# A Fourier mixing and GELU kernel: the spill of the first stage in four parts, and DMA issues held to their slots by tiny transfers

## The chip, the cores and the metric

The kernel runs on one core of one Trainium2 chip. The metric is the device time of one execution in microseconds (us). Before the change it is 1863.5 us, the median of 3 runs (1861.09 to 1864.88). The profile is of a further execution.

## The reference

```python
def _attn_ref(x):                      # x: (8, 3008, 256) float32
    X = np.fft.fft(x, axis=1)
    X = np.fft.fft(X, axis=2)
    return X.real.astype(np.float32)

def _moe_ref(x, w_in, w_out):          # w_in: (256, 2048), w_out: (2048, 256)
    h = x @ w_in
    g = h * (1.0 / (1.0 + np.exp(-1.702 * h)))
    return (g @ w_out).astype(np.float32)

# reference: x = _attn_ref(x).reshape(8 * 3008, 256); return _moe_ref(x, w_in, w_out)
```

For each of 8 batches the real part of a two-dimensional Fourier transform is taken over sequence and channels; each of the 24064 rows then passes a layer with 2048 hidden channels, the sigmoid form of GELU and a second layer.

## The kernel before

**The stages of a batch.** The sequence of 3008 is split as 47 by 64. The **first stage** transforms over the 47: GpSimd folds pairs of rows of the tile xt (`fold1`, lines 208 to 229), TensorE multiplies by tables (`mix1`, line 231), and ScalarE copies the result back into slots of xt (line 256). `mix1` runs in four groups; group m fills the slots 4m to 4m+3 of xt. The result lies in the wrong order for the next stage, so it is written to a scratch tensor Td in DRAM (`spill`, line 326) and read back with other partitions (`fill`, line 331) into the tile t4. `rotate` (line 336) adjusts one column of it, and the **second stage** (`stage2`, line 343) transforms over the 64 for one of three blocks of a batch, into the tile pq. One row of pq goes through DRAM as well (`nyquist_out`, Nd<-pq, line 377) and comes back as a tile nb on all partitions (`nyquist`, line 368).

The input of a batch comes in two ways. `load_x` (line 197) reads it into xt in four pieces, each of two DMAs: one from x itself (512 or 240 KB), one from Xr (as many). Xr holds half of the rows in reversed order and is made by `turn` (line 187), a DMA from DRAM to DRAM in three pieces (752, 705 and 47 KB).

**The main loop.** The two layers are the bulk of the work. They run in 384 steps: 8 batches of 48, and a batch is 3 blocks of 16 steps, each for two of the 16 parts of the hidden channels and a half of a block's columns. In step t, TensorE's `begin` makes the hidden values of the next step in PSUM; ScalarE's `forward` (line 586) applies GELU to the values of step t and writes them into a ring of four places in the tile big (`at_left`, line 518); DVE and ScalarE make the values of the mirrored rows (`backward`, `activate_back`, lines 544 and 593); GpSimd and DVE form sums and differences (lines 601 to 630); TensorE's `product` and `small_products` (lines 182 and 664) multiply them by the second layer's weights three steps later. After 8 steps DVE transposes the results and SyncE stores them (`turned`, `store`, lines 716 and 802). The first 8 steps of batch 0 take a simpler form.

**How the order is set.** The schedule is manual: each engine executes its instructions in the order of the program, and semaphores join the engines. Stages of the next batch are hung into the steps of this one by `at(t, fn, ...)`: the function is called at the end of step t. Below, "slot k" of a batch is step 48b + k. In `begin` and the other functions TensorE, ScalarE, DVE and GpSimd have work in every step, so slots hold them in place. SyncE issues the DMAs, apart from a few at the start and the end, and has an instruction only where a DMA is to be issued. It waits where the data or the place of a DMA isn't ready, or for the completion of the DMA eight places earlier, whose semaphore it uses again; otherwise it goes on to the next DMA in the program's order, whatever its slot. The slots of the moved DMAs in batch b (`late` is 5 in batch 0 and 0 in the others):

- `turn` of batch b+2: slots 11, 12, 13
- `mix1` of batch b+1: slots 11, 15, 19 and 23, plus `late` (one of them a step more in batch 0)
- `spill` of batch b+1: slots 24 and 25, plus `late`; one DMA each for half of the partitions, with 16 slots of xt, 16 KB in one piece for each partition
- `fill` of batch b+1: slots 28, 29, 30, plus `late`
- `load_x` of batch b+2: slots 32, 34, 36, 38, plus `late`
- `rotate` of batch b+1: slot 36 (39 in batch 0); `stage2`: slots 8, 24 and 40, `nyquist_out` and `nyquist` in the two slots behind each

Of the kernel before, what the change touches and what calls it, by code (L numbers as in the profile page):

```python
# [27 lines left out]
F32 = mybir.dt.float32  # L28
# [7 lines left out]
NJ = NB // 2  # L36
NM = 48
# [9 lines left out]
def view(ap, offset, *dims):  # L47
    return bass.AP(ap.tensor, ap.offset + offset, [list(d) for d in dims])
# [63 lines left out]
def kernel(ctx: ExitStack, tc, x, w_in, w_out, tab1, tab2, out):  # L112
    nc = tc.nc
    B, S, D = x.shape
    DF = w_in.shape[1]
    H = D // 2
    NF = DF // 128
    NBLK = NG // 4
# [11 lines left out]

    Xr = [nc.dram_tensor(f"Xr{b}", (NA, NJ, D), F32, kind="Internal").ap() for b in range(B)]
    Nd = nc.dram_tensor("Nd", (B * NBLK, 512), F32, kind="Internal").ap()
    Td = [nc.dram_tensor(f"Td{b}", (NG * 128, D), F32, kind="Internal").ap() for b in range(B)]

    w1 = const.tile([128, (NJ + 3) * NM + 64 - NM], F32, tag="w1", name="w1")
# [15 lines left out]
    big = cv.tile([128, 19 * 1024], F32, tag="big", name="big")  # L151
# [33 lines left out]
    xt = xp.tile([128, NJ, D], F32, tag="x", name="xt")  # L185
# [137 lines left out]
        for _ in range(n):  # L323
            nc.tensor.matmul(ps[:], lhsT=wcs[0][:, 0:128], rhs=wcs[0][:, 0:512], start=True, stop=True)

    def spill(b, c):

        nc.sync.dma_start(out=view(Td[b], 16 * c * D, [NJ * D, NM], [1, 16 * D]),
                          in_=xt[64 * c:64 * c + NM, 0:16, :].rearrange("p q d -> p (q d)"))

    def fill(b, a0=0, a1=NG):
        if a0 == 0:
# [42 lines left out]
    def nyquist_out(b, blk):  # L375
        i = b * NBLK + blk
        nc.sync.dma_start(out=Nd[i:i + 1, :], in_=pqt[b, blk][0:1, 1, :])

    raw = {}

# [109 lines left out]
    A11, A21, S3, S2 = range(4)  # L490
# [27 lines left out]
    def at_left(t, q):  # L518
        return LEFT + t % 4 * 1024 + q * 256
# [311 lines left out]
    for e in odds:  # L831
# [7 lines left out]
                      in_=view(tab1, 0, [tab1.shape[1], 128], [28 * NM, 2], [1, ends]))  # L839
# [70 lines left out]
    def at(t, fn, *args):  # L910
        extra.setdefault(t, []).append((fn, args))
# [22 lines left out]
    for b in range(B):  # L934
        t0 = b * NBLK * NF
        late = 0 if b else 5
        if b + 2 < B:
            for k in range(3):
                at(t0 + 11 + k, turn, b + 2, k)
        if b + 1 < B:  # L940
            for c in range(NCH):
                for part in range(2):
                    at(t0 + 6 + 2 * c + part + late, fold1, b + 1, c, part, nc.gpsimd)
                if c % 2:
                    at(t0 + 9 + 2 * c + late + (late > 0 and c == 5), mix1, b + 1, c // 2)
            for c in range(2):
                at(t0 + 24 + c + late, spill, b + 1, c)
            for blk in range(NBLK):
                at(t0 + 28 + blk + late, fill, b + 1, 4 * blk, 4 * blk + 4)
            if b + 2 < B:  # L950
                for k in range(4):
                    at(t0 + 32 + 2 * k + late, load_x, b + 2, k)
            at(t0 + 36 + 3 * (late > 0), rotate, b + 1)
        for blk in range(NBLK):
            nxt = (b, blk + 1) if blk + 1 < NBLK else (b + 1, 0)
            if nxt[0] < B:
                at(t0 + blk * NF + 8, stage2, *nxt)
                at(t0 + blk * NF + 9, nyquist_out, *nxt)
                at(t0 + blk * NF + 10, nyquist, *nxt)
# [109 lines left out]
```

## Time and profile before

| what | before |
|---|---|
| timed runs, median of 3 | 1863.5 us (1861.09 to 1864.88) |
| profiled execution, its own time | 1870.22 us |
| its span, first to last instruction | 1868.4 us |
| mean granted TensorE clock | 0.998 |
| TensorE matmul busy | 1845.4 us, 99% |
| VectorE (DVE) busy | 1524.2 us, 82% |
| ScalarE (ACT) busy | 1150.3 us, 62% |
| GpSimd (POOL) busy | 962.7 us, 52% |
| SyncE waiting for the transposes ahead of the stores | 1245.3 us |
| bytes moved by DMA | 105.29 MB, mean 56 GB/s |
| DMAs of t<-Td (512 KB), of Td<-xt (768 KB) | 22, 14 |
| DMAs of xt<-x and of xt<-Xr (512 KB, 240 KB) | 14 and 14 of each |

PE is TensorE's matmul, PEld its weight load, which overlaps it. A row of waits names the waiting engine, its output and line, what it waited for, and then the total in us, the times and the longest one; "issue" stands for idle time in which the engine waited for no semaphore that the profile knows. A row of a timeline gives the start and the length in us, the engine, the line, the operation, output<-input and the count. A row of windows gives the stretch, then each engine's busy time with its instructions, the granted clock of TensorE, the mean busy share of the 16 DMA engines and the rate. The DMA view gives for each queue the packets, the megabytes and the share of the 16 engines' time; q1 is SyncE's queue, and the queues of kind "instruction" bring the engines' own instructions.

### The profile page before, as it was taken

How to read it: one execution, taken by the hardware profiler on the slowest of the kernel's cores; microseconds unless marked ns; L12 is line 12 of the kernel's file. 1: busy time of each engine (PE TensorE's matmuls, PEld its weight loads, DVE VectorE, ACT ScalarE, POOL GpSimd, SP SyncE). 2: the span in 40 equal slices, each digit the busy share in tenths (PEclk: the TensorE clock that was granted, in tenths of full speed). 3: DMA queues.
4: the chain of work that ended last, by engine and by line, in shares of the span. 5: the costliest groups of instructions: out<-in, count | busy, mean ns of one | idle time of the engine just before them, and what ended most of it. 6: DMA issues, size and time to landing. Idle time of an engine off the chain costs nothing.

```text
span 1868.4 us, 55818 instructions
## 1 busy us (share of the span) xinstructions
PE 1845.4 (99%) x23684; PEld 1413.1 (76%) x23684; DVE 1524.2 (82%) x2229; ACT 1150.3 (62%) x2248; POOL 962.7 (52%) x1057
## 2 busy tenths in 40 slices
PE   8999999999999999999999999999999999999998
PEld 5677777778777777777777777776877777778776
DVE  7888788888798877987789878887788888878874
ACT  6656666666666656666565666665666666656663
POOL 4676345744367434773348634475335754434442
PEclk9999999999999999999999999999999999999999
DMA  8720351125110350114302251112411021100011
GB/s 262 194 52 17 81 96 32 33 63 107 25 51 14 85 95 14 51 22 113 61 13 61 45 110 31 24 52 63 91 30 25 19 62 35 30 18 14 21 21 24
DMA packets 145690, 105.29 MB, mean 56 GB/s; under 512 B 105163, under 2 KB 128235, under 8 KB 144258
## 3 DMA queue, kind: packets, MB, share of 16 engines
q1 hardware_dynamic: 144226, 101.20, 24.8%
q8 instruction: 187, 3.06, 0.7%
q10 hardware_dynamic: 1216, 0.52, 0.1%
q14 instruction: 61, 0.50, 0.1%
HBM read 64.41 MB, written 48.05 MB: 60 GB/s over the span
## 4 chain that ended last, share of the span: by engine, by line
PE 87%; DVE 6%; ACT 3%; POOL 1%; DMA 1%; issue 1%; SPq 0%; DVEq 0%; ACTq 0%; POOLq 0%
PE x L182 32%; PE o L182 25%; PE low L664 23%; PE o L664 4%; DVE big L630 2%; PE ps L354 1%; PE ps L253 1%; DVE big L765 1%; DVE big L544 1%; DMA big<-in_moe_w_in_dram 1%; ACT x L571 1%; DMA wo<-in_tab_dram 0%; ACT big L586 0%; ACT g L583 0%; PE psw L182 0%
## 5 line engine op out<-in xcount | busy, mean ns | idle before, releaser
L601 POOL TENSOR_TENSOR big<-big 128x256 f32<-128x256 f32 (+1 forms) x376 | 348.2, 926 | 846.5 <-ACT big L593 742.1
L182 PE MATMUL x<-pq,wcs 128*64 128x256 f32 (+1 forms) x6016 | 773.9, 378 | 3.3 <-ACT g L583 2.2
L630 DVE TENSOR_TENSOR big<-big 128x512 f32<-128x512 f32 (+1 forms) x736 | 637.9, 881 | 35.0 <-PE low L664 18.0
L182 PE MATMUL o<-big,wo 128*64 128x256 f32 (+1 forms) x4800 | 623.1, 376 | 0.0
L182 PEld LDWEIGHTS x<-pq,wcs 128*64 128x64 f32 x6016 | 414.4, 137 | 190.7 <-issue 15.0
L182 PEld LDWEIGHTS o<-big,wo 128*64 128x64 f32 x4800 | 344.9, 137 | 144.4 <-DVE big L608 0.5
L583 ACT ACTIVATE g<-x 128x512 f32<-128x512 f32 (+1 forms) x376 | 221.8, 590 | 373.7 <-PE x L182 372.6
L544 DVE TENSOR_TENSOR big<-g,x 128x512 f32<-128x512 f32 (+2 forms) x440 | 253.8, 588 | 200.0 <-ACT big L586 199.7
L664 PE MATMUL low<-big 128*64 128x128 f32 (+1 forms) x5888 | 382.8, 271 | 3.8 <-issue 3.8
L664 PEld LDWEIGHTS low<-big 128*64 128x64 f32 x5888 | 337.8, 137 | 32.2 <-issue 3.9
L571 ACT ACTIVATE x<-nb,af 128x256 f32<-128x256 f32 (+1 forms) x752 | 352.7, 469 | 12.2
L602 POOL TENSOR_TENSOR big<-big 128x256 f32<-128x256 f32 (+1 forms) x376 | 358.8, 954 | 0.0
L586 ACT ACTIVATE big<-x 128x512 f32<-128x512 f32 (+1 forms) x376 | 220.6, 587 | 200.9 <-PE x L182 191.6
L593 ACT ACTIVATE big<-big 128x512 f32<-128x512 f32 (+1 forms) x376 | 231.8, 617 | 42.2 <-DVE big L544 40.3
L664 PE MATMUL low<-big,wo 128*64 128x128 f32 (+1 forms) x2944 | 221.2, 271 | 0.1
L664 PEld LDWEIGHTS low<-big,wo 128*64 128x64 f32 x2944 | 172.9, 137 | 3.8 <-DVE big L630 0.4
L609 DVE TENSOR_TENSOR big<-big 128x512 f32<-128x512 f32 (+1 forms) x188 | 147.7, 786 | 6.5
L608 DVE TENSOR_TENSOR big<-big 128x512 f32<-128x512 f32 (+1 forms) x188 | 136.8, 728 | 5.5 <-POOL big L601 5.5
L765 DVE TENSOR_TENSOR big<-big,low 128x512 f32<-128x512 f32 (+3 forms) x184 | 109.1, 610 | 3.4
L664 PEld LDWEIGHTS o<-big,wo 128*64 128x64 f32 x1472 | 92.7, 137 | 24.5
L664 PE MATMUL o<-big,wo 128*64 128x128 f32 (+1 forms) x1472 | 110.3, 270 | 0.0
L225 POOL TENSOR_TENSOR xt<-xt 111x510 f32<-111x510 f32 x56 | 76.1, 1360 | 4.4
(102 smaller groups left out, 965.8 us busy)
## 6 DMA issues: line engine op xcount, KB each, us to landing
out_dram<-os SPq DMA_DIRECT2D x284, 64.0 KB
t<-Td SPq DMA_DIRECT2D x22, 512.0 KB
Td<-xt SPq DMA_DIRECT2D x14, 768.0 KB
xt<-in_x_dram SPq DMA_DIRECT2D x14, 512.0 KB
xt<-Xr SPq DMA_DIRECT2D x14, 512.0 KB
nb<-Nd SPq DMA_DIRECT2D x23, 256.0 KB
out_dram<-os SPq DMA_DIRECT2D x96, 56.0 KB
Xr<-in_x_dram SPq DMA_DIRECT2D x7, 752.0 KB
```

Source lines behind the costliest of these rows:

```text
L182: nc.tensor.matmul(out[c0:c0 + 64], lhsT=lhs[:, c0:c0 + 64], rhs=rhs, skip_group_check=True, **how)
L544: nc.vector.tensor_tensor(free(out, at + m - 1, [by, 2], [RUN, blocks], [-1, m]), *ins, op=op)
L571: nc.scalar.activation(x[:, i * 256:i * 256 + n], nbt[b, blk][:, hh * 256:hh * 256 + n], ACTF.Copy, scale=af1[:, f:f + 1])
L583: nc.scalar.activation(two(g[:], n), two(xb[t][:], n), ACTF.Copy, scale=2.0)
L586: nc.scalar.activation(front(t), two(xb[t][:], width(t)), ACTF.Gelu_apprx_sigmoid)
L593: nc.scalar.activation(back(t), back(t), ACTF.Gelu_apprx_sigmoid)
L601: eng.tensor_tensor(right(t, S1, n), left(t, A21, n), right(t, A22, n), op=ALU.add)
L602: eng.tensor_tensor(left(t, S3, n), left(t, A11, n), left(t, A21, n), op=ALU.subtract)
L608: eng.tensor_tensor(s2, s1, a11, op=ALU.subtract)
L609: eng.tensor_tensor(s4, a12, s2, op=ALU.subtract)
L630: nc.vector.tensor_tensor(out, i0, i1, op=how)
L664: nc.tensor.matmul(o, lhsT=lhs, rhs=rhs, start=first_in, stop=(p == NP - 2), skip_group_check=True)
```

## The change

The spill is cut in four. `spill` takes a third argument q and moves the four slots of xt that the group q of `mix1` has filled, for half of the partitions, in pieces of 4 KB. Its two DMAs are issued one slot after the group, so that a batch has eight of them at slots 12, 16, 20 and 24 (plus `late`), where it had two.

A new function `paced(t)` issues a DMA of one element: from the place in big that `forward(t)` writes in that step, to a new scratch tensor Tk that nobody reads. SyncE has to wait for `forward(t)` before it issues it, and so do the DMAs behind it. The place is written again by `forward(t + 4)`. A `paced` stands ahead of each `turn`, each `fill` and each `load_x` of the main loop. The fills and the loads have moved one slot forward, to 27, 28, 29 and to 31, 33, 35, 37 (plus `late`).

```diff
+    Tk = nc.dram_tensor("Tk", (B * NBLK * NF, 1), F32, kind="Internal").ap()
...
-    def spill(b, c):
+    def spill(b, c, q):
 
-        nc.sync.dma_start(out=view(Td[b], 16 * c * D, [NJ * D, NM], [1, 16 * D]),
-                          in_=xt[64 * c:64 * c + NM, 0:16, :].rearrange("p q d -> p (q d)"))
+        nc.sync.dma_start(out=view(Td[b], (16 * c + 4 * q) * D, [NJ * D, NM], [1, 4 * D]),
+                          in_=xt[64 * c:64 * c + NM, 4 * q:4 * q + 4, :].rearrange("p q d -> p (q d)"))
...
+    def paced(t):
+        nc.sync.dma_start(out=Tk[t:t + 1, :], in_=big[0:1, at_left(t, A11):at_left(t, A11) + 1])
...
         if b + 2 < B:
             for k in range(3):
+                at(t0 + 11 + k, paced, t0 + 11 + k)
                 at(t0 + 11 + k, turn, b + 2, k)
         if b + 1 < B:
             for c in range(NCH):
                 for part in range(2):
                     at(t0 + 6 + 2 * c + part + late, fold1, b + 1, c, part, nc.gpsimd)
                 if c % 2:
-                    at(t0 + 9 + 2 * c + late + (late > 0 and c == 5), mix1, b + 1, c // 2)
-            for c in range(2):
-                at(t0 + 24 + c + late, spill, b + 1, c)
+                    k = t0 + 9 + 2 * c + late + (late > 0 and c == 5)
+                    at(k, mix1, b + 1, c // 2)
+                    for half in range(2):
+                        at(k + 1, spill, b + 1, half, c // 2)
             for blk in range(NBLK):
-                at(t0 + 28 + blk + late, fill, b + 1, 4 * blk, 4 * blk + 4)
+                at(t0 + 27 + blk + late, paced, t0 + 27 + blk + late)
+                at(t0 + 27 + blk + late, fill, b + 1, 4 * blk, 4 * blk + 4)
             if b + 2 < B:
                 for k in range(4):
-                    at(t0 + 32 + 2 * k + late, load_x, b + 2, k)
+                    at(t0 + 31 + 2 * k + late, paced, t0 + 31 + 2 * k + late)
+                    at(t0 + 31 + 2 * k + late, load_x, b + 2, k)
             at(t0 + 36 + 3 * (late > 0), rotate, b + 1)
```

## The prediction

> **What bounds the kernel now.** I read the page's busy line first, then the chain, then PE's own waits after the start-up, then two stretches of the same work, one batch apart.
>
> ```profile
> PE 1845.4 (99%) x23684; PEld 1413.1 (76%) x23684; DVE 1524.2 (82%) x2229; ACT 1150.3 (62%) x2248; POOL 962.7 (52%) x1057
> ...
> PE 87%; DVE 6%; ACT 3%; POOL 1%; DMA 1%; issue 1%; SPq 0%; DVEq 0%; ACTq 0%; POOLq 0%
> ```
>
> TensorE works 99% of the span and carries the chain, so a DMA edit can give back only what PE loses to a DMA. PE's waits from 85 to 1850 us are three groups (us in total, times, longest):
>
> ```profile
> PE low L664 <- issue: 3.8, 1, 3.8
> PE x L182 <- ACT g L583: 2.2, 6, 0.4
> PE x L182 <- ACT x L571: 0.4, 2, 0.2
> ```
>
> One wait of 3.8 us stands alone, and "issue" means that no semaphore explains it. From the ends of the forward activation (L586) in the trace I took each step's length. Batches 1, 2, 3, 4 and 6 last 225.11 to 225.13 us. Batch 5 lasts 231.78, and the whole 6.66 lies in its steps 25 and 26: 9.99 and 6.00, against 4.63 and 4.70 in the others. The windows show it (PE busy, PEld, DVE, ACT, POOL, granted clock, DMA share, GB/s); the first two rows are batch 5, the others the same work 225.1 us earlier:
>
> ```profile
> 1300.40:1304.20 3.80, 0.04 (x2) 0.03 (x2) 0.00 (x0) 1.81 (x4) 1.40 (x2) 0.84 0.26 89
> 1304.20:1308.80 4.60, 4.60 (x28) 3.90 (x29) 1.35 (x3) 0.60 (x1) 0.00 (x0) 0.50 0.39 119
> ...
> 1075.30:1079.10 3.80, 3.80 (x46) 2.67 (x44) 2.09 (x4) 2.71 (x6) 1.42 (x2) 1.00 0.32 92
> 1079.10:1083.70 4.60, 4.60 (x74) 4.02 (x72) 3.34 (x6) 2.73 (x7) 1.67 (x2) 1.00 0.34 118
> ```
>
> PE stands for 3.8 us and then runs at a granted clock of 0.50 for 4.6 us: 28 matmuls where the other batch has 74. What it waited for is its own instructions. The page counts 187 packets of instructions on q8; in the trace each has 16384 bytes, so one comes every 10 us. From 1282.5 to 1301.5 the DMA view has none:
>
> ```profile
> q8 instruction: 187, 3.06, 0.7%
> ...
> q1 hardware_dynamic: 2055, 2.04, 51.8%
> q14 instruction: 1, 0.01, 0.2%
> ```
>
> The packet due at 1293.0 (they normally start about 0.9 us before PE reaches the 256th instruction after the last) starts at 1302.0, 9.0 late, ends at 1303.0, and PE runs on at 1304.2. SyncE's timeline says what stood in front, and shows the other crowd, the loads of x, which belong to slots 32, 34 and 36 but are issued within 4 us:
>
> ```profile
> 1291.62 0.79 SPq L328 DMA_DIRECT2D Td<-xt  x2
> ...
> 1335.20 0.45 SPq L203 DMA_DIRECT2D xt<-in_x_dram  x1
> 1335.70 0.64 SPq L203 DMA_DIRECT2D xt<-Xr  x1
> 1336.38 0.88 SPq L203 DMA_DIRECT2D xt<-in_x_dram  x1
> 1337.30 0.89 SPq L203 DMA_DIRECT2D xt<-Xr  x1
> 1338.23 0.62 SPq L203 DMA_DIRECT2D xt<-in_x_dram  x1
> 1338.91 0.59 SPq L203 DMA_DIRECT2D xt<-Xr  x1
> ```
>
> Both spills (1.5 MB) were issued 1.4 us before that packet was due; by their semaphores they landed at 1297.9 and 1304.0. The step after the second stage (slot 24) also has short blocks: 256 instructions pass in some 6.3 us there, 8.3 to 10.6 elsewhere, so the late packet had the least time just where the spill lies. Four other packets came with only 0.4 to 0.5 us to spare: one behind a spill (1076.1), three behind the crowd of loads (439.8, 894.4, 1115.7).
>
> [...]
>
> **The change part by part.** Made against the profiled execution: 1870.2 us, its span 1868.4 and 1.8 around it.
>
> PE's instructions, and so the 225.12 us of a clean batch, stay as they are.
>
> Spill: 2 DMAs per batch become 8, in 7 batches 14 become 56, of 192 KB in 4 KB pieces for 768 KB in 16 KB pieces. Six of the eight go out behind the first three mix groups, at slots 12, 16 and 20 (a little later in batch 0), so at slot 24 only 384 KB remain of 1536. The pair took 10.1 to 12.0 us to land in six batches; a quarter of that is 2.5 to 3.0. The short block's 6.3 us, less 1.0 for the packet and 1.2 from its end to PE's restart, leaves 4.1 of room. The stall should be gone: minus 3.8 for the wait and 2.9 for the slow clock, 6.7 by the step lengths.
>
> Loads: 8 DMAs per batch, six batches, one slot earlier by name but held two steps (about 9 us) apart. The largest piece is a pair of 512 KB; 2.5 MB took 19.5 us from 1335.2 to 1354.7, so 1 MB takes about 7.8. The packets with 0.4 us to spare had at least four loads ahead; behind the first pair alone the lateness was 2.7 and 4.4, against 6.1 to 8.4 of room. No stall; nothing is gained in this profile, since none was lost there. Turns: three per batch, six batches, moved from steps 9 to 10 to slots 11 to 13; they landed in 5.6 to 8.5 us, and their readers, the loads, come 18 slots later. Fills: three per batch, seven batches, at 27 to 29; they land in 4.1 to 5.9 and are read at slot 36. All of this is at nothing: the cover is at least 7 steps, 33 us. If it were gone, a late fill would stop PE for its 4 to 6 us.
>
> Tiny transfers: 18 before turns, 21 before fills, 24 before loads, 63 in all. With 42 more spills SyncE issues 105 more DMAs of 0.24 to 0.41 us, under 43 us of an engine that waits 1245 us for the stores. While SyncE waits for forward(t), the move, the stores and the Nd transfers of later slots queue behind it; the stores need later DVE work anyway, and the next row (nb) is wanted some four steps after its slot. In batch 0 the last load shares slot 42 with the nb load, 480 KB ahead of it, about 4 us of 18. On the other side, forward(t+4) rewrites the element read, so ScalarE gets a wait for the transfer's landing. No such read exists in the trace; the nearest is Nd<-pq, 2 KB, 1.1 us to landing and 5.9 at most. From the end of forward(t) to the start of forward(t+4) the slots concerned leave 17.1 us or more, in batch 0's slots 11 and 12 14.7; the longest landing of any DMA after the start-up was 16.8, in the crowd that the change breaks up. Lower bound 0; upper bound, should all 63 land 1 us too late, 63 us. I take 0.
>
> Sum: 1870.2 - 6.7 = 1863.5 for a profiled execution of the changed kernel. The median of the timed runs is already 1863.5 (1861.1 to 1864.9), so how much of the stall they contain is the open size. Spill and packet are locked together: the second spill was issued at the same place in batches 1 to 5 to within 0.03 us, so a timed run meets the same risk. But the lateness varied at like distances (2.8 and 6.6 us at 2.9 and 3.0 after the spill), and the timed runs differ by 3.8, about one wait. Bounds for the gain in timed runs: 0 (none has a stall) and 6.7 (each has it, and the profiling costs as much elsewhere). I take 4.5: the wait and a part of the slow clock.
>
> **The rivals.** (A) The stall is in most timed runs: 1863.5 - 4.5 = 1859.0, own range 1856 to 1859.7. For it: the locked timing and four packets within 0.5 us. (B) The timed runs have little of it: 1861 to 1863.5, no difference. For it: 1870.2 - 6.7 equals the median to 0.1 us, as if only the profiled run stalled. (C) The tiny transfer's landing becomes a wait: ScalarE stops before forward(t+4), and PE behind it. The place is the 24 before loads, the heaviest moves; it decides from a landing of about 17 us, and outweighs A from (4.5 + 3.7) / 24 = 0.34 us of miss each. At 0.5 us each it gives 1863.5 - 4.5 + 12 = 1871; at 1 us, 1883. Against it: a landing came near 17 us only behind six loads at once. (D) The change does not do what it says: forward(t) only holds a DMA from leaving early, and turn and spill meet at slot 12 (705 + 384 KB, some 8 us), or batch 0's load at slot 40 meets a short block; a new stall of 3 to 6.7 takes the place of the old: 1862 to 1866.
>
> **How the numbers follow.** A 0.50, B and D 0.35 together, C and unknown waits 0.15. A difference of 0.2%, 3.7 us, is about what a measurement of this kernel can tell from none. A is mostly faster by more; B and D are within; C is slower. The range runs from 1855.5 (the full 6.7 and 1.3 for near misses) to 1867, into C's mild end.
>
> **What would show it.** In the profile after: no PE wait of "issue" over 1 us, clock 1.00, every batch 225.1 us; 56 spills landing in about 4 us; the load pairs 9 us apart; no packet of instructions over 6 us late; tiny transfers landing within 8 us. Wrong: ScalarE's L586 waiting for a DMA, or PE stalled for issue in slots 11 to 13 or 31 to 42. If the changed kernel's profile takes 1863.5 and its runs do too, B is right.

## The result and the profile after

| | before | after |
|---|---|---|
| timed runs, median of 14 | 1866.92 us | 1862.51 us |
| lowest and highest | 1861.09, 1870.34 | 1861.25, 1864.17 |
| ratio of the times | | 0.9979 (95% interval 0.9969 to 0.9989) |
| profiled execution, its span | 1870.2, 1868.4 us | 1862.0, 1860.2 us |

The changed kernel is 4.4 us faster by the medians, 0.2%. The lowest times are nearly the same. What went is the upper part of the scatter. Of the 14 runs of the kernel before, six lie from 1861.09 to 1864.88 and eight from 1866.79 to 1870.34; after, no run is above 1864.17. The three times shown ahead of the prediction were all from the lower six.

The page's busy line and its chain by engine, after:

```profile
PE 1843.6 (99%) x23684; PEld 1404.9 (76%) x23684; DVE 1522.8 (82%) x2229; ACT 1150.2 (62%) x2248; POOL 963.2 (52%) x1057
...
PE 87%; DVE 6%; ACT 3%; POOL 1%; DMA 1%; issue 1%; SPq 0%; DVEq 0%; ACTq 0%; POOLq 0%
```

The work is the same, matmul for matmul. PE's waits from 85 to 1850 us (total, times, longest), after:

```profile
PE x L183 <- ACT g L587: 2.2, 6, 0.4
PE x L183 <- ACT x L575: 0.4, 2, 0.2
```

The 3.8 us of "issue" are gone, the other two rows are as they were. The windows over the same work in batch 5 (busy time and instructions of PE, PEld, DVE, ACT and POOL, then clock, DMA share and GB/s), after:

```profile
1298.70:1302.50 3.80, 3.80 (x46) 2.66 (x44) 2.08 (x4) 2.71 (x6) 1.42 (x2) 1.00 0.20 66
1302.50:1307.10 4.60, 4.60 (x74) 4.02 (x72) 3.35 (x6) 2.73 (x7) 1.68 (x2) 1.00 0.02 5
```

These are 46 and 74 matmuls at full clock, as in the undisturbed batch of before. In the 19 us that had no packet of instructions there are two now (the DMA view from 1280.8 to 1299.8, after):

```profile
q1 hardware_dynamic: 2156, 1.04, 24.6%
q8 instruction: 2, 0.03, 0.7%
```

and SyncE's timeline shows the short last spill and the held loads:

```profile
1289.90 0.79 SPq L329 DMA_DIRECT2D Td<-xt  x2
...
1326.07 0.29 SPq L381 DMA_DIRECT2D Tk<-big  x1
1326.46 0.33 SPq L204 DMA_DIRECT2D xt<-in_x_dram  x1
1326.84 0.63 SPq L204 DMA_DIRECT2D xt<-Xr  x1
1333.06 0.24 SPq L381 DMA_DIRECT2D Tk<-big  x1
1333.35 0.34 SPq L204 DMA_DIRECT2D xt<-in_x_dram  x1
```

By the step lengths, batches 2 to 6 last 225.12 or 225.13 us and batch 1 225.47. The two profiled spans differ by 8.2 us: 6.7 is the stall of batch 5; 2.1 is the start-up, which the change does not touch (main loop's slot 48 at 276.7 us against 278.8); some 0.5 goes the other way, most of it in batch 1.

### The profile page after: what moved, and what is told of

It reads as the page before. It is cut to its first block, busy times and chain, and to the rows that moved or that the text cites. A ratio compares the mean times of both kernels' runs of the same rounds, so it can differ in the third digit from the quotient of the medians.

```text
span 1860.2 us, 56005 instructions
## 1 busy us (share of the span) xinstructions
PE 1843.6 (99%) x23684; PEld 1404.9 (76%) x23684; DVE 1522.8 (82%) x2229; ACT 1150.2 (62%) x2248; POOL 963.2 (52%) x1057
## 4 chain that ended last, share of the span: by engine, by line
PE 87%; DVE 6%; ACT 3%; POOL 1%; DMA 1%; issue 1%; SPq 0%; DVEq 0%; ACTq 0%; POOLq 0%
PE x L183 32%; PE o L183 24%; PE low L668 23%; PE o L668 4%; DVE big L634 2%; PE ps L355 1%; PE ps L254 1%; DVE big L769 1%; DVE big L548 1%; ACT x L575 1%; DMA big<-in_moe_w_in_dram 1%; ACT big L590 0%; DVE big L612 0%; DMA wo<-in_tab_dram 0%; ACT g L587 0%
## 5 line engine op out<-in xcount | busy, mean ns | idle before, releaser
L183 PEld LDWEIGHTS x<-pq,wcs 128*64 128x64 f32 x6016 | 410.0, 137 | 193.7 <-issue 15.0
```

Of the source, the lines that this page charges most:

```text
L183: nc.tensor.matmul(out[c0:c0 + 64], lhsT=lhs[:, c0:c0 + 64], rhs=rhs, skip_group_check=True, **how)
```

## The experiments

In all of them PE's matmuls from the main loop on are the same; e7 alone has five semaphore instructions fewer on PE. The trace of before has 47868 instructions on PE (23684 matmuls, as many weight loads and 500 others) and 187 packets of 16384 bytes, 256 instructions to a packet. "Late" is the time from when a packet of instructions was due (0.9 us before PE reaches the border of its block of 256, about where undisturbed packets start) to when it starts; it is worked out from the trace's packets. Runs are counted above 1865.4 us, a line over every run of the changed kernel. The kernel before was timed again beside the experiments; with those runs, 102 of its 158 were above that line.

**e1, the spill alone.** The change without `paced`, fills and loads in their old slots.

```diff
+    for half in range(2): at(k + 1, spill, b + 1, half, c // 2)     # as in the change
     at(t0 + 28 + blk + late, fill, ...)                             # no paced, old slots
```

> The spill in four parts behind its mix groups, nothing else: no tiny transfers, fills and loads in their old slots. If the whole spill at slot 24 makes the stall, it goes completely: every run 1861 to 1864.5, median 1862.5, no PE wait of issue in the profile. If the crowd of loads (packets with 0.4 us to spare) stalls PE in other runs as well, a part of the runs stays above 1865 and the median lies at 1863.5 to 1866.

Measured: 1862.53 us (1861.25 to 1863.79), ratio 0.9978 (0.9970 to 0.9985). This is the whole gain. The loads still leave in a crowd, and in the profile a packet behind them was 8.5 us late (before: 7.6 at the same place). PE's waits have:

```profile
PE low L664 <- issue: 0.9, 1, 0.9
```

That batch lasted 226.33 us instead of 225.12. So the crowd takes about 1 us in some executions; the largest that a profile shows is 1.3, in e3.

**e2, the pacing alone.** The tiny transfers and moved slots, with the two old spills at 24 and 25.

> The tiny transfers and the moved fills, loads and turns, but the spill as before: two DMAs of 768 KB at slots 24 and 25. If the spill makes the stall, this is the kernel before again: about half of the runs at 1866.5 to 1870.5, the others at 1861 to 1865. If the crowds of loads and turns make it, all runs lie at 1861 to 1864.5. The tiny transfers alone cost nothing (under 0.5 us) in both.

Measured: 1868.57 us (1861.59 to 1871.11), ratio 1.0003 (0.9991 to 1.0014); 9 of 14 runs above 1865.4. Pacing does nothing to the stall. Its profile has it in batch 5 again, at the same packet, which is 9.0 us late as in the profile before (PE's waits, then three windows):

```profile
PE low L668 <- issue: 4.0, 1, 4.0
```

```profile
1298.30:1302.30 4.00, 0.58 (x8) 0.36 (x5) 0.27 (x1) 1.96 (x4) 1.40 (x2) 0.93 0.31 72
1302.30:1306.90 4.60, 3.99 (x26) 3.46 (x27) 0.70 (x2) 0.60 (x1) 0.00 (x0) 0.50 0.08 23
1306.90:1311.90 5.00, 5.00 (x58) 4.50 (x56) 2.91 (x5) 2.53 (x6) 1.42 (x2) 0.83 0.00 2
```

The batch lasts 232.03 us: 4.0 for the wait, 2.9 for the time at half clock behind it.

**e3, short pieces in the old place.**

```diff
-            at(t0 + 24 + c + late, spill, b + 1, c)
+            for q in range(4): at(t0 + 24 + c + late, spill, b + 1, c, q)
```

> The same 1.5 MB at the same two slots, but in eight DMAs with 4 KB in one piece instead of two with 16 KB; no tiny transfers. If the length of a piece holds the instruction packet back, no run stalls: 1861 to 1864.5. If the bytes queued ahead of it do, the packets come late by 6 to 9 us as before and about half of the runs lie at 1866 to 1870.

Measured: 1863.00 us (1862.03 to 1864.32), ratio 0.9979 (0.9972 to 0.9986). There is no stall behind the spill; the packets due there were at most 2.5 us late, with the same bytes at slot 24. One wait is left, behind the crowd of loads in batch 1, which lasted 226.44 us (PE's waits):

```profile
PE low L664 <- issue: 1.1, 1, 1.1
```

But SyncE needed 7.1 us to issue the eight DMAs, against 0.8 for two, and the pieces of the first groups left 2 us earlier, so the piece length is not the only thing that changed. e9 and e10 take this up.

```profile
1288.80 7.09 SPq L328 DMA_DIRECT2D Td<-xt  x8
```

**e4, the old spill two slots later.**

```diff
-                at(t0 + 24 + c + late, spill, b + 1, c)
+                at(t0 + 26 + c + late, spill, b + 1, c)
```

> The whole spill in two DMAs of 16 KB pieces as before, but at slots 26 and 27, behind the second stage's short block of instructions. If the short block decides, a packet 9 us late finds 6.1 us of room or more, so waits are rare and under 3 us[...]: all runs at 1861 to 1866, median near 1862.5 to 1863.5. If any place is as bad, about half of the runs lie at 1866 to 1870.

Measured: 1862.10 us (1861.16 to 1863.49), ratio 0.9976 (0.9968 to 0.9984). Moving the spill by two slots gives the whole gain. No wait of issue is left in the profile; the packets behind a spill were at most 3.1 us late and met blocks of 10.0 us and more.

**e5 and e6, the border moved, the spill untouched.** Only the warm-up of PE changes; each matmul of the program adds four instructions (the nine of before stand in the trace as 18 matmuls and 18 weight loads).

```diff
-    warm(6)            # of 512 columns
+    warm(30, 96)       # e5: 96 instructions more;  e6: warm(22, 136), 64 more
```

> The kernel before, with the whole spill at slot 24; only the warm-up at the start is 30 matmuls of 96 columns instead of 6 of 512, which puts 96 more instructions ahead of everything on PE and moves every border of 256 instructions. Worked out from the step times, no packet is then due between 0.6 us and 5 us after a spill together with a short block, except one 2.8 us after it in batch 4 (block 7.5 us, like one that came through before). If the meeting of border, spill and short block makes the stall, it is gone with the spill untouched: all runs at 1861 to 1865, median 1862.5 to 1863.5, batch 5 at 225.1 us. If batch 5 stalls for another reason, half of the runs or more lie at 1866 to 1870.

Measured for e5: 1863.60 us (1862.46 to 1865.19), ratio 0.9986 (0.9979 to 0.9993), none of 22 runs above 1865.4. The expectation miscounts one batch: the packet 2.8 us behind a spill is that of batch 3, not 4. It is there in the profile, 7.1 us late, and cost 0.5 us of wait and 0.7 us of the batch's length (PE's waits from 830 to 870 us):

```profile
PE x L182 <- issue: 0.5, 1, 0.5
```

> The same with 22 warm-up matmuls of 136 columns, 64 more instructions on PE. A packet is then due 1.4 us after the spill in batch 1 and 1.8 us after it in batch 5, both with a short block of 6.2 us. If the meeting makes the stall: up to two stalls, runs up to 1875, median 1866 to 1872, and the profile shows the wait in batch 1 or 5 or both. If the border has nothing to do with it, the times are those of the kernel before and batch 5 alone stalls.

Measured for e6: 1869.24 us (1863.04 to 1878.18), ratio 1.0017 (1.0005 to 1.0029), 18 of 22 runs above 1865.4, three above 1876. Here too the text is one batch off: the second packet, 1.8 us behind its spill, belongs to batch 4. There the profile has the stall, and batch 5 lasts 225.13 us (PE's waits, then two windows):

```profile
PE low L664 <- issue: 2.8, 1, 2.8
```

```profile
1074.00:1077.80 3.80, 2.23 (x30) 1.67 (x27) 2.17 (x4) 2.40 (x5) 0.93 (x2) 1.00 0.26 61
1077.80:1082.40 4.60, 3.38 (x19) 2.77 (x20) 0.25 (x1) 0.60 (x1) 0.48 (x1) 0.63 0.57 175
```

Batch 1, where the packet was 4.2 us late, came through in this execution. Together: a few more instructions at the start take the stall away or move it to another batch. It is the meeting of border, spill and short block that makes the large stall, wherever it falls: a wait of 3.8 us in batch 5 of before, of 2.8 in batch 4 of e6.

**e7, a tiny transfer in every step.**

```diff
+    for t in range(NP + 2, n): at(t, paced, t)      # and none ahead of turn, fill, load_x
```

> The changed kernel with a tiny transfer in every step from 10 on, 374 instead of 63. If a tiny transfer costs nothing on the path: 1861 to 1864.5, median 1862.5 as with 63. If the wait for its landing or SyncE's waiting costs something each, 311 more show it sixfold: 0.06 us each would give 1881, 0.02 us 1869.

Measured: 1862.30 us (1860.86 to 1863.63), ratio 0.9976 (0.9967 to 0.9984). The issues in its DMA view and PE's waits:

```profile
Tk<-big SPq DMA_DIRECT2D x374, 0.0 KB
```

```profile
PE x L183 <- ACT g L587: 2.2, 6, 0.4
PE x L183 <- ACT x L575: 0.5, 3, 0.2
```

374 of them cost what 63 cost, nothing that these runs can tell. They landed in 1.0 to 5.9 us, median 1.03; the place they read is free for 14.7 us at the least.

**e8, the old spill twice.** Every spill is followed by the same DMA to another scratch tensor.

> The kernel before with every spill DMA followed by the same DMA to another scratch tensor: 3 MB of 16 KB pieces at slot 24 instead of 1.5. If the queue ahead of the packet sets its lateness, packets in most batches wait until some 20 us after the first spill and PE stalls in three batches or more: 1880 to 1930. If a packet waits for the DMA in front of it only, the times stay near those of the kernel before, 1862 to 1875.

Measured: 1870.70 us (1864.70 to 1876.47), ratio 1.0024 (1.0012 to 1.0037). Far under the 1880 to 1930 expected from a queue that is served to its end. More batches lose time (five of six, 0.3 to 3.4 us each in the profile), but the latest packet was 10.2 us late, against 9.0 with half the bytes, while the four DMAs took up to 21 us to land. PE's waits of issue are several and short:

```profile
PE x L183 <- issue: 3.0, 2, 1.7
...
PE low L665 <- issue: 1.4, 1, 1.4
...
PE o L665 <- issue: 0.8, 1, 0.8
```

This does not show that a packet is served ahead of what is queued, since the 3 MB were not queued at once. SyncE got rid of the first two DMAs in 0.8 us and took 3.3 us for each of the others, so that the packet of batch 5, due about 1.4 us behind the first, had two DMAs ahead of it and the third on its way (SyncE's timeline):

```profile
1295.28 3.28 SPq L329 DMA_DIRECT2D Td<-xt  x1
1298.61 3.38 SPq L329 DMA_DIRECT2D Te<-xt  x1
```

**e9 and e10, how many DMAs and how long a piece.** e9 keeps the 16 KB pieces in six DMAs of 16 partitions; e10 has 4 KB pieces in four DMAs.

```diff
+            for m0 in range(0, NM, 16): at(t0 + 24 + c + late, spill, b + 1, c, m0)   # e9: 16 partitions each
+            for k in range(2): at(t0 + 24 + c + late, spill, b + 1, c, k)             # e10: pieces k and k + 2 of 4 KB
```

> The same spill at slots 24 and 25, in pieces of 16 KB as before, but in six DMAs of 16 partitions (256 KB) instead of two of 48. If the length of a piece makes the packet of instructions wait, the stall stays: a third or more of the runs at 1866 to 1871, median 1865 to 1868. If it is the number of DMAs (the packet gets in between two of them), all runs lie at 1861 to 1865.

Measured for e9: 1863.66 us (1861.96 to 1865.45), ratio 0.9983 (0.9976 to 0.9989), one of 22 runs above 1865.4, by 0.05.

> The same spill at slots 24 and 25 in pieces of 4 KB, in four DMAs (each takes every other group of four slots), fewer than the six of its companion with long pieces. If the length of a piece decides, all runs lie at 1861 to 1865, median about 1863. If the number of DMAs decides, four are between two and eight and a part of the runs stays at 1866 to 1870.

Measured for e10: 1862.85 us (1861.56 to 1864.79), ratio 0.9979 (0.9971 to 0.9987). e9 refutes the length of the piece as the deciding property: with pieces of 16 KB, and the packet of batch 5 due at the same 1.4 us behind the first spill, it was 3.8 us late instead of 9.0. The largest lateness behind a spill falls with the size of one DMA: 9.0 us at 768 KB, 5.2 at 384 (e10), 3.8 at 256 (e9) and 2.5 at 192 (e3); in the changed kernel, with two of 192 KB at a time, it is about 2. The number of DMAs alone is not what helps: e8 had four, of 768 KB, and came to 10.2. Each figure is the largest of a few packets in one profile, and it depends on the place as well, for e4 had 3.1 with 768 KB. With the size goes the time of issue, so that the two aren't told apart (SyncE's timeline of e9):

```profile
1289.67 6.79 SPq L327 DMA_DIRECT2D Td<-xt  x6
```

## Why the prediction was partly right

**What bounds it, and what PE waited for: right.** PE's next block of instructions came late behind the spill at slot 24, which fell together with the second stage's short block. e1, e2 and e4 show the spill, e4 the place, e5 and e6 the border. The sum for the profiled execution, 1863.5, was met to 1.5 us (1862.0); the stall's 6.7 went, and the start-up was 2.1 shorter by chance.

**The size in the timed runs: wrong.** The step that failed is "I take 4.5", the part of the stall that was taken to lie in the median of 1863.5. The runs behind that median held none of it that can be seen: they lie from 1861.09 to 1864.88, and the changed kernel's from 1861.25 to 1864.17. From 1863.5 the change gave 1.0 us, not 4.5, and 1859.0 lies below every run on record. What the runs show in its place is a higher start. The 14 runs put the middle of the kernel before at 1866.9, and their upper group (median 1868.3) lies 6.2 above the lower one (1862.0). Most runs have a stall, by their times: 8 of 14 here and 102 of 158 with the later ones. The three that the prediction had were, as it happened, without one.

The stall's size is not fixed either. In the profiles that have it a batch lost 6.7 us (before), 6.9 (e2) and 4.5 (e6), and the 102 runs fill the stretch from 1865.5 to 1870.95, 3 to 8 us above the changed kernel's median; they spread over 5.5 us, the changed kernel's runs over 2.9. That the medians of the 14 runs differ by 4.4, close to the 4.5, is luck: that number mixes runs with stalls of several sizes and runs with none.

Rival B had said that 1870.2 - 6.7 equals 1863.5; that was the level without a stall, as B read it, and the changed kernel's 1862.5 lies on it. Rival A had the other half: the stall is in most runs. A's gain was set below B's level; the two belonged together, as a gain of up to 6.7 from a higher start to B's time. The working had the warning in it: it called the timed runs' share "the open size" and rested on three runs.

**The near misses: right, and small.** Four packets with 0.4 to 0.5 us to spare were named as risks. e1, where the three behind the crowd of loads stay, lost 1.2 us in one batch of the profile, and e3 1.3, but e1's median (1862.53) is that of the changed kernel. So the pacing of fills, loads and turns, most of the change's lines, brought nothing that these runs can tell. In the changed kernel the least time to spare in the main loop is 2.2 us (3.4 from the packet's end, less the 1.2 that PE took to run on behind the late packet of before).

**The spill's landing: right.** 2.55 to 5.33 us, median 2.68, for "2.5 to 3.0" (the list of signs said "about 4"); the longer ones share slot 12 with a turn, as rival D had it, and the packets there were at most 2.0 us late.

**The tiny transfers at nothing: right.** 1.0 to 4.8 us to landing, for "within 8". The sign that was named is ScalarE's forward waiting for a DMA; the profile has that once, for 0.6 us, and puts it down to a store. From 85 to 1850 us all waits of that line sum to 193.6 us, against 197.0 before. e7 bounds rival C: 311 more transfers changed the median by -0.2 us. No new stall as in rival D was seen in 14 runs.

**The pairs of loads 9 us apart: half right.** 6.9, 9.1 and 16.8 us: the first is held by the stores ahead of it in SyncE's order, the last as well. It made no difference.

**The clock: read too coarsely.** The prediction's rows have PE standing for 3.8 us and then running at 0.50. The same trace has the clock at 0.50 already 2.6 us after PE's last matmul, while PE still waited; the last section shows this.

**What stays open.** Why about a third of the runs of before escape, while both profiled executions with the old spill in its place had the packet 9.0 us late; and why packets due at like times behind a spill wait differently (2.8 us late at 2.8 behind it in batch 1, 6.6 at 3.0 in batch 4, much the same in the profile of e2). The traces' packets narrow it. Where PE stalled in the profiles of before and e2, the instruction packet started as the last of the spill's 96 pieces of 16 KB ended, both at 1302.0 in that of before, 9.0 us after it was due and not until the whole spill had moved. In batches 4 and 6 of the same profile it started with 93 and 96 pieces ended, but in batches 1 and 3 already with 50 and 65. What decides between the two no run here shows.

## What to carry to other kernels

When an engine's only large wait has no semaphore behind it, look for its instruction packets among the DMAs: here two DMAs of 768 KB, issued 1.4 us before a packet was due, at a block of 256 instructions that passes in 6.3 us, stopped for 3.8 us an engine whose other waits from 85 to 1850 us sum to 2.6. Cut such a DMA into several, or move it two steps away from the dense block; either alone was enough here (medians of 1863.00 us in e3 and 1862.10 in e4, beside 1866.80 of the kernel before in the same round), and holding every other transfer to its slot added nothing (1862.51 with it, 1862.53 without, in e1). And if a profiled execution shows a stall that the few timed runs seem not to have, take more runs, and count how many of them have it, before a median is taken as the start.

## What the runs showed of the hardware that was not expected

The latest instruction packet was hardly later with twice the bytes to move: 10.2 us with 3 MB (e8), 9.0 with 1.5. This is no cap that was shown, since in e8 the second half was issued late.

The clock fell in a wait of 2.8 us as it did in the one of 3.8. These windows start where PE's last matmul ended, first in the profile of before, then in that of e6:

```profile
1300.36:1302.96 2.60, 0.00 (x1) 0.00 (x0) 0.00 (x0) 1.85 (x4) 1.40 (x2) 1.00 0.16 54
1302.96:1309.79 6.83, 5.62 (x34) 4.74 (x35) 2.30 (x4) 0.60 (x1) 0.00 (x0) 0.50 0.35 109
```

```profile
1076.23:1078.94 2.71, 0.00 (x0) 0.00 (x0) 0.52 (x1) 1.41 (x4) 1.40 (x2) 1.00 0.25 86
1078.94:1082.36 3.42, 3.34 (x18) 2.75 (x19) 0.21 (x1) 0.60 (x1) 0.00 (x0) 0.50 0.62 181
```

The clock fell 2.6 and 2.7 us after the last matmul (2.9 in e2), stayed at half for 6.8 us in one case and 3.4 in the other, and so made stalls of different size. An estimate from the granted 0.50: half of the 5.6 us that PE was busy at half clock was lost in before, 2.8 on top of the wait of 3.8 (6.7 by the step lengths); half of 3.3 in e6, 1.7 on top of 2.8 (4.5 by the step lengths). In e8 it did not fall: the 4.6 us behind a wait of 1.7 had a granted clock of 1.00.

And the time to issue a DMA is not fixed: two spills of 768 KB took SyncE 0.8 us, but the third and fourth in a row 3.3 and 3.4 each (e8), six of 256 KB 6.8 us and eight of 192 KB 7.1 us.
